# A 2-D spectral filter beside a token MLP: the second transform's radix steps rearranged

## The chip, the cores and the metric

The kernel runs on one core of one Trainium2 chip, as one launch. The metric is the device time in microseconds (us) of a whole execution; the median of three runs is given. The profile is of one execution, and its clock starts at the first recorded instruction.

## The reference, cut to what matters

The input `x` has S = 2048 rows (tokens) and D = 512 columns, in bfloat16.

```python
g = sigmoid((x * gate_w).sum(-1, keepdims=True))
X = rfft2(x.astype(float32)) * (w_r + 1j * w_i)      # 2048 x 257 complex
a = irfft2(X, s=(2048, 512)).astype(bfloat16)
h = layernorm(x)
u = gelu(einsum("bsd,sf->bdf", h, w1) + b1)          # F = 1792
b = (einsum("bdf,fs->bds", u, w2) + b2).transpose(0, 2, 1)
return g * a + (1 - g) * b
```

So there are two branches over the same `x`: a spectral filter (two forward transforms, a product with a complex filter, two inverse transforms) and an MLP over the tokens (two matrix products of 2048 x 1792 x 512 each). A gate per row mixes them.

## The kernel before, in words

**Planner.** Every piece of work is a task with an engine, an estimated duration, what it reads and writes, a priority and the PSUM banks it takes (`Plan`, `add`). A list scheduler (`Plan.order`) runs through time with these estimates and writes out one fixed order for each engine's queue. The chip follows this order; an engine waits at the next instruction until what it reads is there. SP's queue issues nearly all loads and stores.

**MLP.** The first product (`m1`, line 684) accumulates 16 row tiles for each of 14 tiles of F, 512 columns each; ScalarE applies the GELU (line 700). The second (`m2`, line 983) accumulates 14 tiles of F for each of 16 output row tiles; ScalarE or VectorE scale and add them into the output (lines 989, 995, 1001). Weights of the first product stand in a tile `wa` and two tiles `wb`; the second product's weights (14 transfers of 512 KB) are loaded into the same space as it comes free. TensorE is given matmuls of the two products wherever a step of the spectral branch is not ready.

**Spectral branch, forward.** Rows are handled in four residues r of s modulo 4. For each, VectorE does a radix-4 step over row blocks (lines 519 to 526), TensorE multiplies with a cosine and sine table (`fa`, lines 538 to 541; the column d becomes the output's partition, in four blocks `dq`), and ScalarE evicts to the tile `X` (line 544). Then comes the second transform, over the 512 columns. Before the change column d is split as 128 k + p: VectorE does the first radix-4 step over the four blocks k (`d4a`, `d4b`, lines 551 to 558), four instructions for each residue. After that VectorE combines the four residues with a radix-4 step (`radix4`, lines 577 to 590), for each of two halves `lt` of the row frequencies. Half 0 is the special half: one of its columns mixes frequencies and is computed apart with small instructions (`sp0`, `sp1`, lines 602 to 620) and put back into `X` (line 628). Half 1 is combined first.

**Products of the second transform.** For each half, each of four slots `e` and each of two parts c (real and imaginary), a block of four matmuls (`fb`, lines 646 to 649) contracts the partition p: two of 128 columns for the column frequencies 0 and 2 modulo 4, and two of 256 columns that accumulate into one another for the odd ones. That makes 16 blocks. ScalarE evicts each (`fbev`, line 653) into the tile `B` in the order of frequencies. Banks for this come from the two pools `fa` and `fb`, two banks each.

**Filter and inverse.** VectorE prepares small pieces (lines 756 to 793: `wprep`, `c0a`, `c0b`, `nyq`), forms sums and differences (799, 800), multiplies with the filter `W` (807), combines (812 to 821) and does the inverse radix-4 steps (577 to 593). One line goes out by DMA, through a small matmul, and back by DMA. Then the inverse matmuls (`i1`, lines 868 to 875), evictions (881, 883), VectorE sums (891 to 904), the last inverse matmuls (`i3`, lines 942 to 946), evictions with the gate as scale (955) and VectorE's final sums (`es`, lines 964 to 970).

**Gate.** VectorE multiplies `x` with `gate_w` (line 709), ScalarE sums (line 714).

Of the kernel before, what the change touches and what calls it, by code (L numbers as in the profile page):

```python
# [16 lines left out]
P = 128  # L17
S = 2048
D = 512
# [15 lines left out]
def make_tables():  # L35
# [5 lines left out]
    def ang(rows, k, n):  # L41
        return 2 * np.pi * ((rows[..., None] * k) % n) / n
# [42 lines left out]
                    u[:, P] = c[:, P] if lt == 0 else -n[:, P]  # L85
    ti[0, 2816:2945] = np.append(alt, 1.0)

    tb = np.zeros((P, 3, 4, 64))
    i = np.arange(64)
    for b in (0, 2):  # L90
        th = ang(p, b + 4 * i, D)
        tb[:, 0, b // 2] = np.cos(th)
        tb[:, 1, b // 2] = -np.sin(th)
    tb[:, 1, 0, 0] = alt
    tb[:, 2, 0:2] = tb[:, 0, 0:2]
    tc = np.zeros((P, 2, 3, 2, 64))
    for n, b in enumerate((1, 3)):
        th = ang(p, b + 4 * i, D)
        sg = 1.0 if b == 1 else -1.0
        tc[:, 0, 0, n] = np.cos(th)  # L100
        tc[:, 0, 1, n] = -np.sin(th)
        tc[:, 1, 0, n] = -sg * np.sin(th)
        tc[:, 1, 1, n] = -sg * np.cos(th)
    tc[:, :, 2] = tc[:, :, 0]
    cf = np.zeros((P, 4, 2))
    m = np.arange(8).reshape(4, 2)
    for r in range(4):
# [4 lines left out]
            cf[m[2, 0], r, 1], cf[m[3, 0], r, 1] = 1.0, (1.0, -1.0)[r % 2]  # L112
        if r != 0:
            cf[m[2, 1], r, 1], cf[m[3, 1], r, 1] = (0.0, -1.0, 1.0, 1.0)[r], (0.0, -1.0, -1.0, 1.0)[r]
    tb = np.concatenate([tb[:, :, 0:2].reshape(P, 384), tc.reshape(P, 768), cf.reshape(P, 8)], 1)

    tg = np.zeros((P, 642))
    sc = 2.0 / (D * S)
# [21 lines left out]
class Plan:  # L140
# [11 lines left out]
    def add(self, eng, dur, emit, reads=(), writes=(), prio=0.0, alloc=(), free=(), nbytes=0, after=()):  # L152
        t = Task()
        t.eng, t.dur, t.emit, t.prio = eng, dur, emit, prio
        t.alloc, t.free, t.nbytes = tuple(alloc), tuple(free), nbytes
        t.users, t.end, t.ready = [], None, 0.0
        deps = set(after)
        for k in reads:
            if k in self.last_w:
                deps.add(self.last_w[k])  # L160
            self.readers.setdefault(k, []).append(t)
        for k in writes:
            if k in self.last_w:
                deps.add(self.last_w[k])
            deps.update(self.readers.get(k, ()))
            self.last_w[k] = t
            self.readers[k] = []
        deps.discard(t)
        t.deps = deps
        self.tasks.append(t)  # L170
        return t
# [70 lines left out]
def tt(n):  # L242
    return 0.07 + n / 1920.0
# [6 lines left out]
def d1(n):  # L250
    return 0.07 + n / 960.0


def act(n, ptr=0):
    return 0.065 + 0.09 * ptr + n / 1200.0
# [12 lines left out]
def kernel(  # L268
# [77 lines left out]
    def load(key, shape, dt, src, nbytes, prio=0.0):  # L346
        def emit():
            t[key] = sb(shape, dt, key)
            dma(t[key][:], src)
        return add("SP", 0.5, emit, writes=[key], prio=prio, nbytes=nbytes)  # L350
# [52 lines left out]
        dma(t["b1b"][0:NFT], B_b1.rearrange("(t f) -> t f", f=P))  # L403
        dma(t["b2b"][0:4], B_b2.rearrange("(q n) -> q n", q=4))
    add("SP", 1.0, ld_bias, writes=["bias"], prio=7.1, nbytes=16384, after=[a0])
    load("tb", [P, 1160], BF16, tabs["tb"], 296960, prio=9)

    def ld_wb(k, q):
        def emit():
# [46 lines left out]
        dma(t["ti"][:], tabs["ti"])  # L456
    load("tg", [P, 642], BF16, tabs["tg"], 164352, prio=29)


    HACT = set(range(NJ)) - {0, 8, 4}  # L460
    PQ0 = -0.5
    ASTAT = {12, 8}
    for r in range(4):
# [69 lines left out]
        for dq in range(4):  # L533
            def fa(r=r, dq=dq):
                pa = t["pa", r, dq] = ps([P, 2, 2, P], F32, "fa", 2)
                ta = t["ta"][:, r, :]
                w = lambda k: t["xf", r][:, k, dq * P:(dq + 1) * P]
                T.matmul(pa[:, 1], lhsT=w(2), rhs=ta[:, 256:512], start=True, stop=False)  # L538
                T.matmul(pa[:, 1], lhsT=w(3), rhs=ta[:, 384:640], start=False, stop=True)
                T.matmul(pa[:, 0, :, 0:64], lhsT=w(0), rhs=ta[:, 0:128], start=True, stop=True)  # L540
                T.matmul(pa[:, 0, :, 64:128], lhsT=w(1), rhs=ta[:, 128:256], start=True, stop=True)  # L541
            add("PE", mm(128, 128, 256, 256), fa, reads=[("xf", r % 2), ("ta", r)], writes=[("pa", r, dq)], prio=0, alloc=["fa"],
                free=["xf"] if dq == 3 else ())
            add("ACT", act(512), lambda r=r, dq=dq: A.copy(t["X"][:, :, r, :, dq, :], t["pa", r, dq][:]),  # L544
                reads=[("pa", r, dq)], writes=[("X", r, dq)], prio=0, free=["fa"])

        def d4a(r=r):
            xv = t["X"][:, :, r]
            s = t["st"][:, 1024:2048].rearrange("p (a c n) -> p a c n", a=2, c=2)
            two = lambda lo: xv[:, :, :, lo:lo + 2, :].rearrange("p a c j l -> p a c (j l)")  # L550
            V.tensor_add(s, two(0), two(2))
            V.tensor_sub(two(2), two(0), two(2))

        def d4b(r=r):
            xv = t["X"][:, :, r]
            s = t["st"][:, 1024:2048].rearrange("p (a c n) -> p a c n", a=2, c=2)
            V.tensor_add(xv[:, :, :, 0, :], s[:, :, :, 0:P], s[:, :, :, P:2 * P])
            V.tensor_sub(xv[:, :, :, 1, :], s[:, :, :, 0:P], s[:, :, :, P:2 * P])
        add("DVE", 2 * tt(1024), d4a, reads=[], writes=[("X", r, dq) for dq in range(4)] + ["sx"], prio=3.9)
        add("DVE", 2 * tt(512), d4b, reads=["sx"], writes=[("D", r)], prio=3.9)  # L560


    def radix4(view, pq, st, pqk, stk, reads, writes, prio, inverse):
# [56 lines left out]
        V.tensor_add(fx[:, 3, 1], sd[:, 1, 0, 1], sp[:, 2, 1])  # L620
    add("DVE", tiny(12), sp1, reads=["sp"], writes=["fx"], prio=0)

    for lt in (1, 0):
        pr = 3.0 if lt else 3.1
        radix4(lambda lt=lt: t["X"][:, lt].rearrange("p r c j l -> p r c (j l)"),
               lambda: t["xp"][:, 0:2048], lambda: t["st"][:, 0:2048], "xs", "st",
               dk + ([] if lt else ["sp"]), [("Z", lt, 0), ("Z", lt, 1)], pr, False)
    add("DVE", 0.15, lambda: V.tensor_copy(t["X"][:, 0, :, :, :, 0], t["fx"][:]), reads=["fx"],
        writes=[("Z", 0, 0), ("Z", 0, 1)], prio=3.1)

    def tbl(kind, c):
        tb = t["tb"]
        if kind < 2:
            return tb[:, 0:384].rearrange("p (c k i) -> p c k i", c=3, k=2)[:, c:c + 2, kind, :]
        v = tb[:, 384:1152].rearrange("p (g n) -> p g n", g=2)[:, kind - 2]
        return v[:, 128 * c:128 * c + 256]

    for lt in (0, 1):
        for e in (0, 2, 1, 3):
            for c in range(2):  # L640
                tag = ("fa", "fb")[c]

                def fb(lt=lt, e=e, c=c, tag=tag):
                    pb = t["pb", lt, e, c] = ps([P, 2, 4, 64], F32, tag, 2)
                    w = lambda k: t["X"][:, lt, e, c, k, :]
                    T.matmul(pb[:, :, 0, :], lhsT=w(0), rhs=tbl(0, c), start=True, stop=True)
                    T.matmul(pb[:, :, 2, :], lhsT=w(1), rhs=tbl(1, c), start=True, stop=True)
                    for k in (2, 3):
                        T.matmul(pb[:, :, 1::2, :], lhsT=w(k), rhs=tbl(k, c), start=(k == 2), stop=(k == 3))
                add("PE", mm(128, 128, 256, 256), fb, reads=[("Z", lt, e % 2), "tb"], writes=[("pb", lt, e, c)], prio=2, alloc=[tag])  # L650

                def fbev(lt=lt, e=e, c=c):
                    A.copy(t["B"][:, lt, e, 2 * c:2 * c + 2, :].rearrange("p s (i b) -> p s i b", b=4),  # L653
                           t["pb", lt, e, c][:].rearrange("p s b i -> p s i b"))
                add("ACT", act(512), fbev, reads=[("pb", lt, e, c)], writes=[("B", lt, e)], prio=1.8, free=[tag])


    def biasT():
# [105 lines left out]
    for lt in range(2):  # L764
# [8 lines left out]
        if lt == 0:  # L773
            def nyq():
                pz = sb([1, 1280], F32, "X")
                na = pz[:, 0:1024].rearrange("p (i v l) -> p i v l", i=2, v=2)
                nn = t["nn"] = pz[:, 1024:1280].bitcast(BF16).rearrange("p (v l) -> p v l", v=2)
                wn, v = t["wn"], t["B"][0:1, 0, 0, 2:4, :]
                for i in range(2):
                    V.tensor_mul(na[:, i], v, wn[:, i, None, 0:L].to_broadcast([1, 2, L]))  # L780
                V.tensor_sub(nn[:, 0], na[:, 0, 1], na[:, 1, 0])
                V.tensor_add(nn[:, 1], na[:, 1, 1], na[:, 0, 0])
                V.tensor_mul(nn[:, :, 0], t["c0"][0:1, 0, 0, 1, :], wn[:, 0, 0:257:256])
            add("DVE", 3 * d1(512) + 0.1, nyq, reads=bk + [("W", 0), ("W", 1), ("c0", 0)] + pbk, writes=["nn"], prio=0.5)

        def c0b(lt=lt):
            c0, cm, ce, pm = t["c0"][:, lt], t["cm"], t["ce"][:, lt], t["wpm"]
# [46 lines left out]

    def linem():
        pl8 = t["pl8"] = ps([8, D], F32, "fa", 2)
        T.matmul(pl8[:], lhsT=t["tb"][:, 1152:1160], rhs=t["s9"][:], start=True, stop=True)
    add("PE", mm(512), linem, reads=["s9", "tb"], writes=["pl8"], prio=3, alloc=["fa"], after=[combt])
    add("ACT", act(512), lambda: A.copy(t["s8"][:], t["pl8"][:]), reads=["pl8"], writes=["s8"], prio=1.7, free=["fa"])

# [205 lines left out]
```

## Time and profile before

| what | value |
|---|---|
| time, three runs | 132.38, 132.47, 134.06 us, median 132.47 |
| profiled execution | 132.39 us, of which span 130.5 us |
| granted TensorE clock | 0.997 |
| TensorE busy | 125.4 us, 96% |
| VectorE busy | 110.6 us, 85% |
| ScalarE busy | 83.1 us, 64% |
| moved by DMA | 23.18 MB |

The span runs from the first to the last recorded instruction; the execution's time has 1.9 us more around it. A timeline line has start, time, engine, line, operation, output and inputs with their shapes, and in square brackets the idle time of the engine just before and what ended it. Matmuls are pipelined: a recorded matmul of 512 columns lasts 379 ns while the next one starts about 216 ns after it, so distances between starts are what a matmul costs in a stream. The same holds for short VectorE and ScalarE instructions: their starts are closer than their durations.

### The profile page before, as it was taken

How to read it: one execution, taken by the hardware profiler on the slowest of the kernel's cores; microseconds unless marked ns; L12 is line 12 of the kernel's file. 1: busy time of each engine (PE TensorE's matmuls, PEld its weight loads, DVE VectorE, ACT ScalarE, POOL GpSimd, SP SyncE). 2: the span in 40 equal slices, each digit the busy share in tenths (PEclk: the TensorE clock that was granted, in tenths of full speed). 3: DMA queues.
4: the chain of work that ended last, by engine and by line, in shares of the span. 5: the costliest groups of instructions: out<-in, count | busy, mean ns of one | idle time of the engine just before them, and what ended most of it. 6: DMA issues, size and time to landing. Idle time of an engine off the chain costs nothing.

```text
span 130.5 us, 2166 instructions
## 1 busy us (share of the span) xinstructions
PE 125.4 (96%) x780; PEld 70.7 (54%) x780; DVE 110.6 (85%) x248; ACT 83.1 (64%) x166; POOL 0.2 (0%) x4
## 2 busy tenths in 40 slices
PE   6998999999999999999999999999999999999991
PEld 2344565545544484854444555455687577655590
DVE  2689999999999997059999999999959929999961
ACT  4468989599999999996111044322499489962200
POOL 0000000000000000000000000000000000000000
PEclk9999999999999999999999999999999999999998
DMA  4999999943669536799999800000000000312331
GB/s 83 389 372 386 398 394 379 374 91 89 135 184 298 107 85 131 259 288 406 414 421 421 334 6 0 3 5 3 0 0 0 0 5 0 161 69 97 161 121 40
DMA packets 17478, 23.18 MB, mean 178 GB/s; under 512 B 1574, under 2 KB 14908, under 8 KB 17468
## 3 DMA queue, kind: packets, MB, share of 16 engines
q1 hardware_dynamic: 17180, 22.59, 50.6%
q10 hardware_dynamic: 288, 0.46, 1.3%
q8 instruction: 6, 0.10, 0.3%
q14 instruction: 4, 0.03, 0.1%
HBM read 20.93 MB, written 2.10 MB: 176 GB/s over the span
## 4 chain that ended last, share of the span: by engine, by line
PE 58%; DVE 28%; DMA 8%; issue 2%; ACT 2%; SPq 0%; DVEq 0%
PE acc L684 18%; PE acc L983 17%; DMA wa<-in_B_w_dram 5%; PE fb L684 5%; DVE xp L807 3%; DVE st L807 3%; DMA x<-in_A_x_dram 2%; PE fa L684 2%; PE fa L538 2%; DVE xp L812 2%; DVE st L578 2%; DVE B L819 2%; DVE xp L813 2%; PE fb L868 1%; PE fa L868 1%
## 5 line engine op out<-in xcount | busy, mean ns | idle before, releaser
L983 PE MATMUL acc<-gl,wb 128*128 128x512 bf16 (+1 forms) x112 | 27.4, 373 | 0.0
L983 PE MATMUL acc<-gl,wa 128*128 128x512 bf16 (+1 forms) x112 | 27.2, 372 | 0.0
L684 PE MATMUL acc<-h,wb 128*128 128x512 bf16 x112 | 25.9, 379 | 0.0
L989 ACT ACTIVATE x<-acc,ombb,omg 128x512 bf16<-128x512 f32 x14 | 10.8, 785 | 22.7 <-PE acc L983 22.7
L983 PEld LDWEIGHTS <-wb 128*128 128x128 bf16 x126 | 13.4, 114 | 10.3 <-DMA wb<-in_B_w_dram 1.2
L983 PEld LDWEIGHTS <-wa 128*128 128x128 bf16 x126 | 13.5, 114 | 9.4
L684 PE MATMUL acc<-h,wa 128*128 128x512 bf16 x64 | 17.8, 387 | 0.6 <-DVE h L505 0.6
L684 PEld LDWEIGHTS <-wb 128*128 128x128 bf16 x112 | 10.9, 98 | 11.7
L684 PEld LDWEIGHTS <-wa 128*128 128x128 bf16 x112 | 10.4, 99 | 10.8 <-issue 2.1
L700 ACT ACTIVATE gl<-acc,b1f 128x512 bf16<-128x512 f32 x11 | 7.6, 693 | 6.8 <-PE acc L684 6.8
L478 DVE BATCH_NORM_STATS2 stats<-x 128x6 f32<-128x512 bf16 x14 | 9.4, 674 | 2.2 <-DMA x<-in_A_x_dram 2.2
L544 ACT CAST X<-fa 128x512 bf16<-128x512 f32 x16 | 9.3, 582 | 2.7 <-PE fa L541 2.5
L511 ACT ACTIVATE h<-x,nmr,rstd 128x512 bf16<-128x512 bf16 x13 | 9.8, 806 | 0.4 <-DVE nmr L502 0.2
L714 ACT ACTIVATE x<-x 128x512 bf16<-128x512 bf16 x16 | 10.1, 655 | 0.0
L684 PE MATMUL fb<-h,wa 128*128 128x512 bf16 x32 | 9.4, 379 | 0.0
L955 ACT ACTIVATE B<-fb,g 128x512 bf16<-128x512 f32 x8 | 5.9, 735 | 0.0
L955 ACT ACTIVATE B<-fa,g 128x512 bf16<-128x512 f32 x8 | 5.8, 727 | 0.0
L359 PE MATMUL fa<-xp 128*128 128x512 bf16 x10 | 4.4, 632 | 1.2 <-DVE xp L320 1.2
L684 PE MATMUL fa<-h,wa 128*128 128x512 bf16 x16 | 5.6, 379 | 0.0
L653 ACT CAST B<-fb 128x512 bf16<-128x512 f32 x8 | 5.0, 628 | 0.0
L653 ACT CAST B<-fa 128x512 bf16<-128x512 f32 x8 | 4.9, 616 | 0.0
L709 DVE TENSOR_TENSOR x<-x,gw 128x2048 bf16<-128x2048 bf16 x4 | 4.8, 1216 | 0.0
(177 smaller groups left out, 230.0 us busy)
## 6 DMA issues: line engine op xcount, KB each, us to landing
wb<-in_B_w_dram SPq DMA_DIRECT2D x11, 512.0 KB
wa<-in_B_w_dram SPq DMA_DIRECT2D x7, 512.0 KB
wa<-in_B_w_dram SPq DMA_DIRECT2D x3, 896.0 KB
x<-in_A_x_dram SPq DMA_DIRECT2D x3, 512.0 KB
wb<-in_B_w_dram SPq DMA_DIRECT2D x4, 384.0 KB
out_dram<-x SPq DMA_DIRECT2D x3, 512.0 KB
rot<-dft_ti SPq DMA_DIRECT2D x1, 736.5 KB
rot<-dft_ta SPq DMA_DIRECT2D x4, 160.0 KB
```

Source lines behind the costliest of these rows:

```text
L478: V.bn_stats(out=t["stats"][:, j, :], in_=t["x"][:, j // 4, j % 4, :])
L511: add("ACT", 0.71, lambda j=j: A.activation(t["h"][:, j // 4, j % 4, :], t["x"][:, j // 4, j % 4, :], ActF.Identity, bias=t["nmr"][:, j:j ...
L544: add("ACT", act(512), lambda r=r, dq=dq: A.copy(t["X"][:, :, r, :, dq, :], t["pa", r, dq][:]), reads=[("pa", r, dq)], writes=[("X", r, dq ...
L653: A.copy(t["B"][:, lt, e, 2 * c:2 * c + 2, :].rearrange("p s (i b) -> p s i b", b=4), t["pb", lt, e, c][:].rearrange("p s b i -> p s i b"))
L684: T.matmul(t["u", ft][:], lhsT=w[:, j // 4, j % 4, c * P:(c + 1) * P], rhs=t["h"][:, j // 4, j % 4, :], start=(j == jorder[0]), stop=(j == ...
L700: gelus.append(add("ACT", act(512, 1) , lambda ft=ft: A.activation(t["gl"][:, ft, :], t["u", ft][:], ActF.Gelu_apprx_tanh, bias=t["b1f"][: ...
L709: add("DVE", tt(2048), lambda r=r: V.tensor_mul(t["x"][:, :, r, :], t["x"][:, :, r, :], t["gw"][:, None, :].to_broadcast([P, 4, D])), read ...
L714: A.activation(t["x"][:, q, r, :], t["x"][:, q, r, :], ActF.Copy, accum_out=t["glog"][:, 4 * q + r:4 * q + r + 1])
L807: V.tensor_mul(o, xs, w)
L955: A.activation(t["eo", j // 2][:, j % 2], t["i3", j][:], ActF.Copy, scale=t["g"][:, j:j + 1])
L983: T.matmul(t["y", j, n][:, cs], lhsT=w[:, o, 512 * q + r:512 * q + 512:4], rhs=t["gl"][:, ft, cs], start=(ft == 0), stop=(ft == NFT - 1))
L989: A.activation(tbuf(j).rearrange("p h d -> p (h d)"), t["y", j, 0][:], ActF.Identity, bias=t["ombb2"][:, j:j + 1], scale=t["omg"][:, j:j + 1])
```

## The change

Column d is split as 256 h + 2 p + t, with h and t 0 or 1. The first transform takes its stationary operand at every second column, so that its blocks are (h, t). Its evictions go to the scratch tile `xp`, and VectorE does a radix-2 step over h from `xp` to `X` (`d2`), in place of the radix-4 step over k. The products have four matmuls of 128 columns per block, one for each t and each parity of the frequency; each gives cosine and sine parts of 64 frequencies, with which the mirrored frequencies are built as well. The evictions write them interleaved over the products' own operands in `X`, and wait for both blocks of a pair. VectorE then does a radix-2 step over t, from `X` to `B` (`tb2`: three instructions for the even slots of a half, six for the odd ones). The special half is combined first and put first. The table `tb` shrinks from 1160 to 776 columns.

```diff
     load("tb", ...)
-    [P, 1160], 296960 bytes
+    [P, 776], 198656 bytes
...
+    def xe(r):
+        return t["xp"][:, 2048 * r:2048 * r + 2048].rearrange("p (a c j l) -> p a c j l", a=2, c=2, j=4)
...
-                w = lambda k: t["xf", r][:, k, dq * P:(dq + 1) * P]
+                w = lambda k: t["xf", r][:, k, L * (dq // 2) + dq % 2:L * (dq // 2 + 1):2]
...
-            add("ACT", act(512), lambda r=r, dq=dq: A.copy(t["X"][:, :, r, :, dq, :], t["pa", r, dq][:]),
+            add("ACT", act(512), lambda r=r, dq=dq: A.copy(xe(r)[:, :, :, dq, :], t["pa", r, dq][:]),
...
-            V.tensor_add(s, two(0), two(2))
-            V.tensor_sub(two(2), two(0), two(2))
...
-            V.tensor_add(xv[:, :, :, 0, :], s[:, :, :, 0:P], s[:, :, :, P:2 * P])
-            V.tensor_sub(xv[:, :, :, 1, :], s[:, :, :, 0:P], s[:, :, :, P:2 * P])
...
+        def d2(r=r):
+            e, xv = xe(r), t["X"][:, :, r]
+            for i in range(2):
+                V.tensor_add(xv[:, i, :, 0:2], e[:, i, :, 0:2], e[:, i, :, 2:4])
+                V.tensor_sub(xv[:, i, :, 2:4], e[:, i, :, 0:2], e[:, i, :, 2:4])
...
-    for lt in (1, 0):
-        pr = 3.0 if lt else 3.1
+    for lt in (0, 1):
+        pr = 3.0 + 0.1 * lt
...
-                    T.matmul(pb[:, :, 0, :], lhsT=w(0), rhs=tbl(0, c), start=True, stop=True)
-                    T.matmul(pb[:, :, 2, :], lhsT=w(1), rhs=tbl(1, c), start=True, stop=True)
-                    for k in (2, 3):
-                        T.matmul(pb[:, :, 1::2, :], lhsT=w(k), rhs=tbl(k, c), start=(k == 2), stop=(k == 3))
+                    for k in range(4):
+                        T.matmul(pb[:, k % 2, :, k // 2, :], lhsT=t["X"][:, lt, e, c, k, :], rhs=tbl(k, c), start=True, stop=True)
...
-                    A.copy(t["B"][:, lt, e, 2 * c:2 * c + 2, :].rearrange("p s (i b) -> p s i b", b=4),
-                           t["pb", lt, e, c][:].rearrange("p s b i -> p s i b"))
+                    A.copy(t["X"][:, lt, e].rearrange("p c j l -> p (c j l)").rearrange("p (h c g) -> p h c g", h=2, c=2)[:, :, c]
+                           .rearrange("p h (s i b) -> p h s b i", s=2, b=2), t["pb", lt, e, c][:])
...
+            if e >= 2:
+                def tb2(lt=lt, e0=e - 2):
+                    b = t["B"][:, lt]
+                    v = t["X"][:, lt].rearrange("p e c j l -> p e (c j l)").rearrange("p e (h w l) -> p e h w l", h=2, w=4)
+                    bh, vh = b[:, e0::2], v[:, e0::2]
+                    V.tensor_add(bh[:, :, :, 0:P], vh[:, :, 0], vh[:, :, 1])
+                    V.tensor_sub(bh[:, :, 0:4:3, L - 1:P:-1], vh[:, :, 0, 0:4:3, 1:P], vh[:, :, 1, 0:4:3, 1:P])
+                    V.tensor_sub(bh[:, :, 1:3, L - 1:P:-1], vh[:, :, 1, 1:3, 1:P], vh[:, :, 0, 1:3, 1:P])
+                    if e0:
+                        V.tensor_sub(b[:, :, 1:3, 0], v[:, :, 0, 0:4:3, 0], v[:, :, 1, 0:4:3, 0])
+                        V.tensor_copy(b[:, :, 0:4:3, P], v[:, :, 0, 1:3, 0])
+                        V.tensor_copy(b[:, :, 1:3, P], v[:, :, 1, 1:3, 0])
```

In the changed kernel the radix 2 over h stands at lines 545 and 546, the products at line 630, their evictions at line 637 and the radix 2 over t at lines 646 to 652.

More of the change, by code (lines that the diff above doesn't have):

```diff
@@ L86, in make_tables @@
     ti[0, 2816:2945] = np.append(alt, 1.0)
[L88 to L104, printed above, removed]
+    tb = np.zeros((P, 2, 2, 3, 64))
+    for par in range(2):
+        for h in range(2):
+            th = ang(2 * p + h, par + 2 * np.arange(64), D)
+            tb[:, par, h, 0] = np.cos(th)
+            tb[:, par, h, 1] = -np.sin(th)
+            if par == 0:
+                tb[:, 0, h, 1, 0] = (alt, -alt)[h]
+            tb[:, par, h, 2] = tb[:, par, h, 0]
     cf = np.zeros((P, 4, 2))
@@ L114, in make_tables @@
             cf[m[2, 1], r, 1], cf[m[3, 1], r, 1] = (0.0, -1.0, 1.0, 1.0)[r], (0.0, -1.0, -1.0, 1.0)[r]
-    tb = np.concatenate([tb[:, :, 0:2].reshape(P, 384), tc.reshape(P, 768), cf.reshape(P, 8)], 1)
+    tb = np.concatenate([tb.reshape(P, 768), cf.reshape(P, 8)], 1)
     tg = np.zeros((P, 642))
@@ L405 @@
     add("SP", 1.0, ld_bias, writes=["bias"], prio=7.1, nbytes=16384, after=[a0])
-    load("tb", [P, 1160], BF16, tabs["tb"], 296960, prio=9)
+    load("tb", [P, 776], BF16, tabs["tb"], 198656, prio=9)
     def ld_wb(k, q):
@@ L543 @@
                 free=["xf"] if dq == 3 else ())
-            add("ACT", act(512), lambda r=r, dq=dq: A.copy(t["X"][:, :, r, :, dq, :], t["pa", r, dq][:]),
+            add("ACT", act(512), lambda r=r, dq=dq: A.copy(xe(r)[:, :, :, dq, :], t["pa", r, dq][:]),
                 reads=[("pa", r, dq)], writes=[("X", r, dq)], prio=0, free=["fa"])
[L547 to L550, printed above, removed]
-            V.tensor_add(s, two(0), two(2))
-            V.tensor_sub(two(2), two(0), two(2))
-        def d4b(r=r):
-            xv = t["X"][:, :, r]
-            s = t["st"][:, 1024:2048].rearrange("p (a c n) -> p a c n", a=2, c=2)
-            V.tensor_add(xv[:, :, :, 0, :], s[:, :, :, 0:P], s[:, :, :, P:2 * P])
-            V.tensor_sub(xv[:, :, :, 1, :], s[:, :, :, 0:P], s[:, :, :, P:2 * P])
-        add("DVE", 2 * tt(1024), d4a, reads=[], writes=[("X", r, dq) for dq in range(4)] + ["sx"], prio=3.9)
-        add("DVE", 2 * tt(512), d4b, reads=["sx"], writes=[("D", r)], prio=3.9)
+        def d2(r=r):
[3 more added lines that the diff above has]
+                V.tensor_sub(xv[:, i, :, 2:4], e[:, i, :, 0:2], e[:, i, :, 2:4])
+        add("DVE", 4 * tt(512), d2, reads=[("X", r, dq) for dq in range(4)], writes=[("D", r)], prio=3.9)
     def radix4(view, pq, st, pqk, stk, reads, writes, prio, inverse):
@@ L627 @@
                dk + ([] if lt else ["sp"]), [("Z", lt, 0), ("Z", lt, 1)], pr, False)
-    add("DVE", 0.15, lambda: V.tensor_copy(t["X"][:, 0, :, :, :, 0], t["fx"][:]), reads=["fx"],
-        writes=[("Z", 0, 0), ("Z", 0, 1)], prio=3.1)
+        if lt == 0:
+            add("DVE", 0.15, lambda: V.tensor_copy(t["X"][:, 0, :, :, :, 0], t["fx"][:]), reads=["fx"],
+                writes=[("Z", 0, 0), ("Z", 0, 1)], prio=3.0)
     def tbl(kind, c):
[L632 to L636, printed above, removed]
+        return t["tb"][:, 192 * kind + 64 * c:192 * kind + 64 * c + P].rearrange("p (s i) -> p s i", s=2)
     for lt in (0, 1):
@@ L643, in fb @@
                 def fb(lt=lt, e=e, c=c, tag=tag):
[L644 to L647, printed above, removed]
-                    for k in (2, 3):
-                        T.matmul(pb[:, :, 1::2, :], lhsT=w(k), rhs=tbl(k, c), start=(k == 2), stop=(k == 3))
@@ L650 @@
-                add("PE", mm(128, 128, 256, 256), fb, reads=[("Z", lt, e % 2), "tb"], writes=[("pb", lt, e, c)], prio=2, alloc=[tag])
-                def fbev(lt=lt, e=e, c=c):
-                    A.copy(t["B"][:, lt, e, 2 * c:2 * c + 2, :].rearrange("p s (i b) -> p s i b", b=4),
-                           t["pb", lt, e, c][:].rearrange("p s b i -> p s i b"))
-                add("ACT", act(512), fbev, reads=[("pb", lt, e, c)], writes=[("B", lt, e)], prio=1.8, free=[tag])
+                    pb = t["pb", lt, e, c] = ps([P, 2, 2, 2, 64], F32, tag, 2)
@@ new lines, in fb @@
+                    for k in range(4):
+                        T.matmul(pb[:, k % 2, :, k // 2, :], lhsT=t["X"][:, lt, e, c, k, :], rhs=tbl(k, c), start=True, stop=True)
+                add("PE", mm(128, 128, 128, 128), fb, reads=[("Z", lt, e % 2), "tb"], writes=[("pb", lt, e, c)], prio=2, alloc=[tag])
+            for c in range(2):
+                tag = ("fa", "fb")[c]
+                def fbev(lt=lt, e=e, c=c):
+                    A.copy(t["X"][:, lt, e].rearrange("p c j l -> p (c j l)").rearrange("p (h c g) -> p h c g", h=2, c=2)[:, :, c]
+                           .rearrange("p h (s i b) -> p h s b i", s=2, b=2), t["pb", lt, e, c][:])
+                add("ACT", act(512), fbev, reads=[("pb", lt, e, i) for i in range(2)], writes=[("R", lt, e, c)], prio=1.8, free=[tag])
@@ new lines @@
+            if e >= 2:
[10 more added lines that the diff above has]
+                        V.tensor_copy(b[:, :, 1:3, P], v[:, :, 1, 1:3, 0])
+                es_ = (e - 2, e) if e == 2 else (0, 1, 2, 3)
+                add("DVE", tt(1024) + 2 * tt(508) + tiny(3) * (e > 2), tb2, reads=[("R", lt, i, c) for i in (e - 2, e) for c in range(2)],
+                    writes=[("B", lt, i) for i in es_], prio=2.5)
@@ L783, in nyq @@
                 V.tensor_mul(nn[:, :, 0], t["c0"][0:1, 0, 0, 1, :], wn[:, 0, 0:257:256])
-            add("DVE", 3 * d1(512) + 0.1, nyq, reads=bk + [("W", 0), ("W", 1), ("c0", 0)] + pbk, writes=["nn"], prio=0.5)
+            add("DVE", 3 * d1(512) + 0.1, nyq, reads=[("B", i, e) for i in range(2) for e in range(4)] + [("W", 0), ("W", 1), ("c0", 0)] + pbk, writes=["nn"], prio=0.5)
         def c0b(lt=lt):
@@ L836, in linem @@
         pl8 = t["pl8"] = ps([8, D], F32, "fa", 2)
-        T.matmul(pl8[:], lhsT=t["tb"][:, 1152:1160], rhs=t["s9"][:], start=True, stop=True)
+        T.matmul(pl8[:], lhsT=t["tb"][:, 768:776], rhs=t["s9"][:], start=True, stop=True)
     add("PE", mm(512), linem, reads=["s9", "tb"], writes=["pl8"], prio=3, alloc=["fa"], after=[combt])
```

## The prediction

> **What bounds the kernel now.** First the busy times and slices of the page, to see which engine has no idle time.
>
> ```profile
> span 130.5 us, 2166 instructions
> ...
> PE 125.4 (96%) x780; PEld 70.7 (54%) x780; DVE 110.6 (85%) x248; ACT 83.1 (64%) x166; POOL 0.2 (0%) x4
> ...
> PE   6998999999999999999999999999999999999991
> ...
> DVE  2689999999999997059999999999959929999961
> ```
>
> TensorE is busy in every slice, and a busy figure can hide a slow stream, so the PE timeline is read next: how far apart do the matmuls start?
>
> ```profile
> 45.42 0.22 PE L646 MATMUL fa<-tb,X 128*128 128x128 bf16 x1
> 45.48 0.22 PE L647 MATMUL fa<-tb,X 128*128 128x128 bf16 x1
> 45.53 0.38 PE L649 MATMUL fa<-tb,X 128*128 128x256 bf16 x2
> 45.75 0.22 PE L646 MATMUL fb<-tb,X 128*128 128x128 bf16 x1
> ...
> 104.70 0.22 PE L942 MATMUL fa<-tg,xp 128*128 128x129 bf16 x1
> ...
> 105.82 0.38 PE L983 MATMUL acc<-gl,wa 128*128 128x512 bf16 x1
> ...
> 116.75 1.67 PE L983 MATMUL acc<-gl,wb 128*128 128x512 bf16 x7
> 118.26 1.67 PE L983 MATMUL acc<-gl,wa 128*128 128x512 bf16 x7
> ```
>
> One block of the second transform takes 0.33 us (45.42 to 45.75). Between 104.70 and 105.82 stand twenty matmuls of 127 to 129 columns: 0.056 us each. Seven matmuls of 512 columns take 1.51 us, 0.2155 each. Starts lie as close as columns allow, almost everywhere, so the end is set by the number of columns that TensorE streams. Work taken from it shortens the span, if its fixed order never waits. Two other views show who could make it wait, the DVE timeline and that of the weight loads.
>
> ```profile
> 51.40 0.25 DVE L628 CAST X<-fx 128x32 bf16<-128x32 f32 x1
> 56.51 0.17 DVE L770 CAST c<-B 128x8 f32<-128x8 bf16 x1 [4.86 <-ACT B L653]
> ...
> 126.03 0.48 DVE L1001 SCALAR_TENSOR_TENSOR x<-acc,omg,x 128x256 bf16<-128x256 f32 x1 [0.75 <-PE acc L983]
> ```
>
> ```profile
> 69.74 0.11 PEld L983 LDWEIGHTS <-wb 128*128 128x128 bf16 x1 [0.30 <-DMA wb<-in_B_w_dram]
> ...
> 70.97 0.11 PEld L983 LDWEIGHTS <-wb 128*128 128x128 bf16 x1 [0.43 <-DMA wb<-in_B_w_dram]
> ```
>
> VectorE is nearly full, but stands idle 4.86 us while ScalarE evicts the special half, and at the end it has 0.75 us to spare before TensorE's last outputs. At 69 to 71 us the second MLP product uses weight tiles the moment they land.
>
> **The products, TensorE.** Each of 16 blocks loses its two 256-column matmuls for two of 128. Four of 128 at 0.056 make 0.224 for 0.33: 0.106 x 16 = 1.70 us off the path. The operands of the first transform are now read at stride 2 as weights; the inverse transform's weights (L868) are read at stride 2 already and load in 98 ns, as do contiguous ones (98 ns at L538): nothing. The nearest bound from the other side is that one 98 ns load per matmul could not be hidden: 4 x 0.098 = 0.39 per block, +1.0 us. I take 0.056, since all twenty matmuls above have such a load each.
>
> The Trainium skill speaks against this edit: TensorE: Matmul & The Clock Gate, section Back-to-back issue gap, gives about 81 ns for each of a sustained stream of weight load and 128-column matmul. By it a block would keep 0.324 us, and TensorE would gain an estimated 0.1 us. The trace has 56 ns in such a stream and does not agree.
>
> **VectorE.** The old radix 4 over column blocks takes two instructions of 1024 and two of 512 elements per row residue: 2.00 us from start to start (25.19 to 27.46, less 0.27 of other work). The new radix 2 takes four of 512, at 0.335 (L557, L558): 1.34. Four residues: -2.6 us. Added is the radix 2 over t behind the products, four times: one of 1024 (0.60, as L583) and two of 508 (0.335 start to start, as L967 and L968, which also read from an odd element and one of which writes backwards), and twice three tiny ones of 0.075: 4 x 1.27 + 0.45 = 5.5 us. Net +2.9 us on an engine with 19.9 us idle.
>
> Where does it fall? The built order puts all four L709 multiplies ahead of the last residue's radix 2, and three 512-column matmuls more ahead of that residue's last block (35.59 + 0.65 = 36.24), so its eviction ends near 37.4 and the radix 2 near 38.85, where the old one ended at 40.00. From 40.00 to the first product with the filter (63.81) VectorE is busy 18.3 us and idle 5.5, all waits for evictions. With the special half first, the evictions run from 46 to 54 while VectorE still has the other half's radix 4, so the idle time fills: 38.85 + 18.3 + 5.5 = 62.65, 1.15 us earlier than before. From there the chain is unchanged, so its end comes 1.15 earlier, with 0.75 to spare before: it stays behind TensorE for a gain up to 1.9.
>
> **The special half first.** TensorE reaches the first block after the same 77 matmuls of the first MLP product, at 45.42. It now needs the special column as well: 38.85 + 0.2 copy + 1.0 (twelve tiny ones) + 2.27 + 1.2 + 1.2 (radix 4) + 0.35 (column put back) = 45.07. Cover 0.35 us; without it TensorE and all MLP matmuls queued behind stand still, one for one.
>
> **Evictions.** Still 16 of 512, now waiting for both blocks of a pair (0.22 us, once), as they overwrite the products' operands. They start 0.477 apart (L653, 45.95 to 49.29). The 5th to 8th block need banks at 46.75, 47.19, 47.63 and 48.07, freed at 46.6, 47.1, 47.55 and 48.03: 0 to 0.2 us of waits. New is that each writes every second element. No row has such a write. Bounds: 0.477 from L653, which reads as scattered, and 0.71 from L989, the dearest of that size (three in 2.12). I take L653, the same engine, size and source.
>
> The Trainium skill has a price for the stride: SBUF — State Buffer, section Door 1: The DMA port swizzle, has 16-byte lines and full speed from two hits a line on; two-byte values at stride 2 hit four times, so by it the eviction costs nothing more. No run here shows it yet.
>
> **Transfers.** SP issues the same list in the same order; the table is 98 KB smaller, at 390 GB/s (the page's early slices) 0.25 us. But the tiles of the second weight matrix come at the pace of the DMA engines (busy share 0.94 to 1.0 from 53 to 74 us), whatever TensorE does. It would start that product at 68.02 - 1.70 = 66.32. The built order uses the second wb tile as its 14th matmul, at 69.12; that tile let go at 69.74 before. Waits of 0.4 to 0.7 us against 0.2 before (31 matmuls took 6.87, not 6.68): -0.2 to -0.5 of the gain, 0.35 taken. Behind that tile everything on TensorE queues, so it is not made up. The inverse transform needs VectorE and the line sent back by DMA (90.8 at the latest by the shift of 1.15, TensorE there at about 92): covered.
>
> **Sum.** 1.70 - 0.35 = 1.35 us. The profiled execution took 132.39 (span 130.5 and 1.9 around it): 131.04. The median is 0.08 above the profiled one: 131.1.
>
> **Rivals.** First, *waits eat the gain*: TensorE's fixed order waits for the radix 4 at 45.4 and 51.6 (cover 0.35 and 0.2), for banks, and for tiles. For it: all covers are below 0.4. Against: the order was moved along with the work. With 0.5 at each of two places, 132.1.
>
> Second, the other side, *slow interleaved evictions make VectorE the bound*. The third of the added radix-2 steps needs twelve evictions and one activation, done at 52.3, where VectorE can take it at 52.65. If a write at stride 2 takes twice the time (0.95), they are done at 58.0, VectorE's chain comes 5.35 later less 1.15, and past its 0.75 to spare the end goes to 132.4 + 4.2 - 0.75 = 135.9. VectorE decides from 0.56 us an eviction, and the kernel is slower than before from 0.67. At L989's 0.71 it is 0.5 slower: 132.9. For it: nothing measured writes so. Against: ScalarE's 512-element rows differ only by 0.1 with layout (L544 to L653).
>
> Third, *weight loads pace the products*, so the change does not do what it says: 132.4 + 1.0 = 133.4. Against: the twenty matmuls.
>
> By the 81 ns of the Trainium skill (TensorE: Matmul & The Clock Gate, Back-to-back issue gap) this third way would give an estimated 132.3.
>
> **Chances.** Forecast 0.62 (own range 130.4 to 131.7); waits 0.17; evictions 0.13, of which 0.09 past 2%; weight loads 0.04; a gain beyond 2% 0.04, for waits that the trace hides. Two per cent of the median is 2.65 us, about what a measurement of this kernel can tell from no change. So faster 0.04, slower 0.10 (evictions 0.09 and 0.01 for weight loads with waits on top), within 0.86. The range runs from 130.3 (no wait at all is 130.7, plus the table's 0.25 and a little) to 133.4.
>
> **What would show it.** Right: products 0.056 apart; evictions still 0.477 apart and ending near 54.5; no VectorE idle time of several us between 39 and 63; filter products from about 62.6; first wb tiles waited for about 0.5 us; TensorE ending 1.3 us sooner. Wrong: eviction groups above 700 ns mean, 508-element steps far above 0.42, PE rows with waits for VectorE, or VectorE busy to the last store.

## The result, and the profile after

The changed kernel takes 133.68 us (median of 17 runs, 133.53 to 133.91) against 132.46 before (17 runs): a ratio of 1.0085, 95% interval 1.007 to 1.0101. It is slower by 1.2 us, where 131.1 was forecast and 133.4 was the end of the range. That is within the 2% by which the prediction tells faster and slower apart, and yet clear of noise: the interval is 0.15% (0.2 us) wide on each side. The top of its page:

```profile
span 131.7 us, 2172 instructions
...
PE 124.1 (94%) x766; PEld 69.6 (53%) x780; DVE 113.8 (86%) x266; ACT 84.9 (64%) x166; POOL 0.2 (0%) x4
...
PE   6899999999999999869999999999999999999991
```

TensorE has less to do and the span is longer: the 17th and 18th of the 40 slices (52.7 to 59.3 us) show 8 and 6 tenths where the kernel before had nines. That is the stretch of the products and their evictions. The PE timeline of the changed kernel there (idle time in brackets):

```profile
45.65 0.39 PE L630 MATMUL fa<-tb,X 128*128 128x128 bf16 x4
45.87 0.39 PE L630 MATMUL fb<-tb,X 128*128 128x128 bf16 x4
...
54.58 0.39 PE L630 MATMUL fb<-tb,X 128*128 128x128 bf16 x4 [0.35 <-ACT X L637]
...
57.39 0.38 PE L736 MATMUL fb<-wt,flip 128*128 128x256 bf16 x2 [0.92 <-ACT X L637]
...
69.52 1.68 PE L983 MATMUL acc<-gl,wa 128*128 128x512 bf16 x7
```

A block takes 0.22 us as forecast. But TensorE waits for ScalarE to free banks. From the first product to the second MLP product (45.65 to 69.52) it needs 23.87 us for work of 20.68 (16 blocks of 0.222, 77 matmuls at 0.2155, and an estimated 0.54 for the filter's flips): 3.2 us lost. Before, 45.42 to 68.02 held work of 22.41, and 0.2 was lost. So 1.7 us of work was saved and 3.0 us of waits came. Another 0.2 came ahead of the first product (45.65 for 45.42), so that the second MLP product starts 1.5 us later. Behind that point 0.3 comes back: the last group of matmuls starts at 128.21 for 127.00, 1.2 us later.

The page's groups of evictions (this one and its twin from the pool `fa`, of 778 ns) and the ScalarE timeline of the changed kernel show who is late:

```profile
L637 ACT CAST X<-fb 128x512 bf16<-128x512 f32 x8 | 6.3, 784 | 1.5 <-DVE B L648 1.5
```

```profile
46.23 0.75 ACT L637 CAST X<-fa 128x512 bf16<-128x512 f32 x1
46.81 0.76 ACT L637 CAST X<-fb 128x512 bf16<-128x512 f32 x1
...
49.13 0.81 ACT L637 CAST X<-fb 128x512 bf16<-128x512 f32 x1
...
52.62 0.74 ACT L637 CAST X<-fa 128x512 bf16<-128x512 f32 x1 [0.30 <-DVE X L577]
...
54.36 0.76 ACT L637 CAST X<-fa 128x512 bf16<-128x512 f32 x1
56.61 0.73 ACT L637 CAST X<-fb 128x512 bf16<-128x512 f32 x1 [1.49 <-DVE B L648]
```

Two things are seen. Evictions start 0.58 apart, not 0.477. And ScalarE stands still for VectorE, in the middle of them. The VectorE timeline has the other side:

```profile
49.97 0.69 DVE L646 TENSOR_TENSOR B<-X 128x1024 bf16<-128x1024 bf16 x1 [1.09 <-ACT X L637]
...
55.16 0.69 DVE L646 TENSOR_TENSOR B<-X 128x1024 bf16<-128x1024 bf16 x1 [1.09 <-ACT X L637]
...
56.10 0.42 DVE L648 TENSOR_TENSOR B<-X 128x508 bf16<-128x508 bf16 x1
```

The first radix-2 step over t reads slots 0 and 2, which evictions 1 to 4 write; the fourth ends at 48.76 (47.97 + 0.79). The step starts at 49.97, when the sixth ends (49.13 + 0.81), which writes slot 1. The third step, of the other half, starts at 55.16, when the 13th ends (54.36 + 0.76), again slot 1. In return the 14th, slot 1 too, waits until that step's last instruction ends (56.10 + 0.42). No value passes between them. The reading is that the program's waits take a slice of every second slot as all that lies between its first and its last, so that a step over slots 0 and 2 and an eviction into slot 1 wait for one another; a run below tests it. The 11th eviction (slot 2) waits likewise for the radix 4 that writes slots 1 and 3 (L577, done at 51.85 + 0.69).

### The profile page after: what moved, and what is told of

Its sections match the earlier page's. It is cut to its first block, busy times and chain, and to the rows that moved or that the text cites. A ratio compares the mean times of both kernels' runs of the same rounds, so it can differ in the third digit from the quotient of the medians.

```text
span 131.7 us, 2172 instructions
## 1 busy us (share of the span) xinstructions
PE 124.1 (94%) x766; PEld 69.6 (53%) x780; DVE 113.8 (86%) x266; ACT 84.9 (64%) x166; POOL 0.2 (0%) x4
## 4 chain that ended last, share of the span: by engine, by line
PE 70%; ACT 17%; DVE 6%; DMA 2%; issue 1%; ACTq 0%
PE acc L983 35%; PE acc L684 17%; ACT X L637 5%; ACT x L714 4%; ACT gl L700 4%; PE fb L684 3%; DMA x<-in_A_x_dram 2%; PE fa L684 2%; PE fa L533 2%; ACT xp L539 2%; PE fb L868 1%; PE fa L868 1%; DVE B L646 1%; PE fa L534 1%; ACT W L740 1%
## 5 line engine op out<-in xcount | busy, mean ns | idle before, releaser
L684 PE MATMUL acc<-h,wb 128*128 128x512 bf16 x108 | 25.3, 379 | 0.2
L684 PE MATMUL acc<-h,wa 128*128 128x512 bf16 x61 | 17.2, 389 | 0.8 <-DVE h L500 0.6
L539 ACT CAST xp<-fa 128x512 bf16<-128x512 f32 x16 | 9.3, 580 | 3.0 <-PE fa L536 2.8
L637 ACT CAST X<-fb 128x512 bf16<-128x512 f32 x8 | 6.3, 784 | 1.5 <-DVE B L648 1.5
L637 ACT CAST X<-fa 128x512 bf16<-128x512 f32 x8 | 6.2, 778 | 0.3 <-DVE X L577 0.3
L630 PEld LDWEIGHTS <-X 128*128 128x128 bf16 x64 | 4.4, 97 | 3.3 <-issue 2.3
```

Source lines behind the costliest of these rows:

```text
L539: add("ACT", act(512), lambda r=r, dq=dq: A.copy(xe(r)[:, :, :, dq, :], t["pa", r, dq][:]), reads=[("pa", r, dq)], writes=[("X", r, dq)], ...
L630: T.matmul(pb[:, k % 2, :, k // 2, :], lhsT=t["X"][:, lt, e, c, k, :], rhs=tbl(k, c), start=True, stop=True)
L637: A.copy(t["X"][:, lt, e].rearrange("p c j l -> p (c j l)").rearrange("p (h c g) -> p h c g", h=2, c=2)[:, :, c] .rearrange("p h (s i b) - ...
L684: T.matmul(t["u", ft][:], lhsT=w[:, j // 4, j % 4, c * P:(c + 1) * P], rhs=t["h"][:, j // 4, j % 4, :], start=(j == jorder[0]), stop=(j == ...
```

## The experiments

Theory A: TensorE's fixed order waits for banks, for two separate reasons, the slower eviction and these waits between neighbours. Theory B, the rival: VectorE's longer chain costs the time. That TensorE's waits are for banks is read from what ended them, ScalarE's evictions; no run gave the products more banks. All runs of one group shared the runs of the kernel before (medians 132.45 and 132.47).

**Evictions that write in one piece.** Only the eviction's order of elements is changed: PSUM is now read scattered.

```diff
-    .rearrange("p h (s i b) -> p h s b i", s=2, b=2), t["pb", lt, e, c][:])
+    .rearrange("p h (s i b) -> p h s i b", s=2, b=2), t["pb", lt, e, c][:].rearrange("p h s b i -> p h s i b"))
```

> The changed kernel, but its 16 evictions of the products read PSUM scattered and write SBUF in one piece, instead of reading in one piece and writing every second element; the values and the orders of all queues stay the same. Theory A (the lost time is TensorE waiting for banks in its fixed order, for two reasons: each eviction costs 0.58 instead of 0.477 us, and the radix 2 over t and the evictions wait for one another where they touch different slots): starts of evictions 0.477 apart again, TensorE's loss between the first product and the first matmul of the second MLP product falls from 3.2 to about 1.5 us, time 131.8 to 132.4. Theory B (the longer VectorE chain is what costs): evictions may be faster, but the time stays at 133.3 or above.

Measured: 132.44 us, ratio 0.9999 (0.9989 to 1.001), 1.24 us less than the changed kernel and just above the 131.8 to 132.4 that was expected. Evictions start 0.477 apart. TensorE's loss is 1.9 us, more than the 1.5 expected; the waits between neighbours stay. ScalarE's timeline of this run:

```profile
46.85 0.63 ACT L637 CAST X<-fb 128x512 bf16<-128x512 f32 x1
47.33 0.64 ACT L637 CAST X<-fa 128x512 bf16<-128x512 f32 x1
...
52.11 0.59 ACT L637 CAST X<-fa 128x512 bf16<-128x512 f32 x1 [0.74 <-DVE X L577]
...
55.74 0.59 ACT L637 CAST X<-fb 128x512 bf16<-128x512 f32 x1 [1.49 <-PE fa L736]
```

The second wait is put down to TensorE's L736 here. That matmul, started at 55.33, writes other banks than this eviction reads; the eviction's own block was started at 52.21. VectorE's last instruction of the step over slots 0 and 2 ends at 55.65, just ahead of 55.74:

```profile
55.23 0.42 DVE L648 TENSOR_TENSOR B<-X 128x508 bf16<-128x508 bf16 x1
```

**Neighbouring slots.** The forward radix 4 writes its results in the order 0, 2, 1, 3, so that a step over t reads two slots that lie side by side.

```diff
-            V.tensor_sub(dst(4, 1), p, q)
+            V.tensor_sub(dst(4 if inverse else 2, 1), p, q)
...
-                V.tensor_add(dst(2, 5), s, ur)
-                V.tensor_sub(dst(3, 3), sr, u)
+                V.tensor_add(dst(4, 3), s, ur)
+                V.tensor_sub(dst(5, 1), sr, u)
...
-                    bh, vh = b[:, e0::2], v[:, e0::2]
+                    bh, vh = b[:, e0::2], v[:, 2 * e0:2 * e0 + 2]
```

The products and the evictions use slot 2 (e % 2) + e // 2 as well, and the special column is put back accordingly.

> The changed kernel, but the forward radix 4 puts slot 2 next to slot 0 and slot 3 next to slot 1, so that the radix 2 over t reads two neighbouring slots and no longer spans the slot between them; evictions still write every second element. Theory A: the waits of ScalarE for VectorE (1.49 and 0.30 us) and of VectorE for the fifth, sixth and thirteenth eviction go, evictions stay 0.58 apart, time 132.2 to 133.0. Theory B: 133.3 or above.

Measured: 131.86 us, ratio 0.9949 (0.9935 to 0.9964), 1.82 less than the changed kernel and a little better than expected. The evictions that waited run through, still 0.58 apart; these two in the ScalarE timeline are the 13th and the 14th:

```profile
53.79 0.88 ACT L641 CAST X<-fa 128x512 bf16<-128x512 f32 x1
54.36 0.90 ACT L641 CAST X<-fb 128x512 bf16<-128x512 f32 x1
```

**Both edits.**

> The changed kernel with both of these edits. Theory A: what was forecast for the change comes out, 130.8 to 131.5, with TensorE's loss between the first product and the second MLP product below 0.6 us and waits for the second weight matrix of about 0.4 us in their place. Theory B: the time stays above 132.9, since VectorE has the same work.

Measured: 130.63 us (130.38 to 130.79), ratio 0.9854 (0.9835 to 0.9873). This is 1.8 us (1.5%) faster than the kernel before, within the 2% but clear of noise, a little better than expected, and 3.05 faster than the changed one; the two edits alone gave 1.24 and 1.82, which add up to 3.06. Theory A holds and B falls: VectorE has the same work as in the changed kernel. The waits of 0.4 us for the second weight matrix that were expected did not come. Lines of this run's PE and weight-load timelines, one fence each:

```profile
45.90 0.39 PE L634 MATMUL fa<-tb,X 128*128 128x128 bf16 x4
...
66.68 1.67 PE L989 MATMUL acc<-gl,wa 128*128 128x512 bf16 x7
```

```profile
68.09 0.11 PEld L989 LDWEIGHTS <-wb 128*128 128x128 bf16 x1 [0.22 <-DMA wb<-in_B_w_dram]
```

| kernel | evictions apart | TensorE lost, 1st product to 2nd MLP product | filter products from | time |
|---|---|---|---|---|
| before | 0.477 | 0.2 | 63.81 | 132.46 |
| changed | 0.58 | 3.2 | 65.33 | 133.68 |
| in one piece | 0.477 | 1.9 | 64.16 | 132.44 |
| neighbouring slots | 0.58 | 1.3 | 63.87 | 131.86 |
| both | 0.477 | 0.1 | 62.82 | 130.63 |

**The eviction's write in the kernel before.** There the frequencies are interleaved by four.

```diff
-    A.copy(t["B"][:, lt, e, 2 * c:2 * c + 2, :].rearrange("p s (i b) -> p s i b", b=4),
-           t["pb", lt, e, c][:].rearrange("p s b i -> p s i b"))
+    A.copy(t["B"][:, lt, e, 2 * c:2 * c + 2, :].rearrange("p s (i b) -> p s b i", b=4), t["pb", lt, e, c][:])
```

> The kernel before, but its 16 evictions of the products read PSUM in one piece and write every fourth element of SBUF, instead of the other way round. Theory A: the cost of an eviction follows the write, so starts are 0.58 apart or more instead of 0.477, and the kernel loses some of the 1.7 us that ScalarE needs more: 132.8 to 133.8. If the cost belongs to something else in the changed kernel (an access in more dimensions, or writing over the products' operands), evictions stay at 0.477 and the time at 132.4.

Measured: 142.7 us, ratio 1.077 (1.075 to 1.079), far beyond what theory A expected: the direction is the expected one, the size is not. The ScalarE timeline:

```profile
46.93 1.40 ACT L653 CAST B<-fb 128x512 bf16<-128x512 f32 x1
48.06 1.41 ACT L653 CAST B<-fa 128x512 bf16<-128x512 f32 x1
49.21 1.40 ACT L653 CAST B<-fb 128x512 bf16<-128x512 f32 x1
```

At every fourth element an eviction takes 1.14 us from start to start, 2.4 times the one in one piece. Sixteen of them cost ScalarE 10.6 us more, and the kernel pays 10.2. The cost belongs to the write, not to the changed kernel's place or dimensions: the edit in the changed kernel kept both and came back to 0.477.

**The special half last again,** with both edits.

```diff
-    for lt in (0, 1):
-        pr = 3.0 + 0.1 * lt
+    for lt in (1, 0):
+        pr = 3.1 - 0.1 * lt
```

> The kernel with both edits, but with the special half combined last again, as before the change. Theory A: this step is worth something only as cover: VectorE again waits some microseconds for the last evictions, and since its chain has no spare time left at the end, the kernel is 0.5 to 2 us slower than with both edits, 131.1 to 132.6. If the order of the halves does not matter, 130.5 to 130.8.

Measured: 134.88 us, ratio 1.0197 (1.0173 to 1.0221): 4.25 us slower than both edits with the special half first, twice what was expected at most. The planner makes new orders here, so the step is measured together with what else moves by it. VectorE's timeline:

```profile
56.54 0.69 DVE L650 TENSOR_TENSOR B<-X 128x1024 bf16<-128x1024 bf16 x1 [3.87 <-ACT X L641]
58.50 0.69 DVE L650 TENSOR_TENSOR B<-X 128x1024 bf16<-128x1024 bf16 x1 [0.59 <-ACT X L641]
...
129.42 0.34 DVE L1007 SCALAR_TENSOR_TENSOR x<-fb,omg,x 128x128 bf16<-128x128 f32 x1
```

VectorE waits 4.5 us for evictions, its filter products start at 66.96 instead of 62.82, and at the end it works without a pause to 129.8, while TensorE's last group starts at 125.45, as in the run with both edits (125.37). Here VectorE sets the end.

**The special half first, alone,** in the kernel before.

```diff
-    for lt in (1, 0):
-        pr = 3.0 if lt else 3.1
+    for lt in (0, 1):
+        pr = 3.0 + 0.1 * lt
```

The special column is put back right after its own half, as in the change.

> The kernel before with this one step of the change: the special half combined first and put first. Theory A: VectorE's wait of 4.86 us for evictions shrinks and its filter products start earlier than 63.81, but TensorE's columns set the end, so the time stays within 0.4 of 132.45. If VectorE's chain were what sets the end, it would fall by a microsecond or more.

Measured: 132.22 us, ratio 0.9996 (0.997 to 1.0022): no difference. VectorE's longest wait there shrinks from 4.86 to 1.56 us and its filter products start at 61.84, but the time stays, as it should where TensorE sets the end. The step is worth nothing where VectorE has time to spare, and about 4 us where it has none.

**One addition of VectorE twice,** with both edits.

```diff
-                    V.tensor_add(bh[:, :, :, 0:P], vh[:, :, 0], vh[:, :, 1])
+                    for _ in range(2):
+                        V.tensor_add(bh[:, :, :, 0:P], vh[:, :, 0], vh[:, :, 1])
```

> The kernel with both edits, with the 1024-element addition of each of the four radix-2 steps over t done twice (the second time over the same values): 2.4 us more for VectorE, nothing else. It measures what VectorE has to spare. If VectorE's work is hidden as the forecast had it (spare up to about 0.5 us at the end), the time rises by 1.5 to 2.4, to 132.1 to 133.0; if VectorE still has several microseconds to spare, it stays at 130.6 to 131.0.

Measured: 133.52 us, ratio 1.0082 (1.0068 to 1.0096), 2.9 more than without for 2.4 us of work, somewhat above what was expected. The PE timeline shows where it surfaces, at the inverse transform:

```profile
93.40 0.22 PE L879 MATMUL fa<-rot,B 128*128 128x129 bf16 x1 [1.53 <-DMA B<-s]
...
96.36 0.23 PE L879 MATMUL fb<-rot,B 128*128 128x128 bf16 x1 [0.97 <-DVE B L580]
```

TensorE waits 2.5 us, for the line sent back by DMA (itself behind VectorE) and for the inverse radix 4. With both edits alone, the DVE and PE timelines show the same radix 4 and the matmul behind it:

```profile
93.07 0.68 DVE L580 TENSOR_TENSOR B<-st 128x1024 bf16<-128x1024 bf16 x1
```

```profile
93.81 0.23 PE L878 MATMUL fb<-rot,B 128*128 128x128 bf16 x1
```

The radix 4 ends at 93.75 and the matmul starts at 93.81: TensorE and VectorE are due together there, and VectorE has nothing to spare. The matmul is 2.55 us later with the doubled addition (96.36 for 93.81), and the two profiled executions are 2.6 apart (133.40 and 130.79). The 2.9 of the medians has 0.3 more only because these two executions lie at the near ends of their runs.

## Why the prediction was wrong, by its steps

**The products (1.70 us): right.** Blocks of 0.22 us. The first sixteen of the 64 matmuls, in one stream with a weight load each, take 0.89 us (45.65 to 46.54), 0.0555 us each; the 81 ns of the Trainium skill (TensorE: Matmul & The Clock Gate, Back-to-back issue gap) is not what this kernel shows.

**VectorE's work: right.** The radix 2 over h took 1.34 us (25.24 to 26.58), the steps over t 0.60 and twice 0.335, the special column was put back at 45.1 to 45.35 where 45.07 was worked out, ahead of the first product at 45.65. (The prediction's 77 matmuls of the first MLP product are those behind the first product; 147 stand ahead of it, in both kernels.) With both edits the filter products start at 62.82; 62.65 was forecast.

**The evictions: this step failed, twice.** First the price: 0.477 was taken from L653 since it was nearest, and it is 0.58 when every second element is written. The bounds of 0.477 and 0.71 held it, and the prediction's own sign of being wrong, eviction groups above 700 ns mean, came true at 778 and 784. The rival on the other side named the slow write. But it gave 0.67 us as the point from which the kernel is slower, through VectorE's end, while at 0.58 the loss already came, through banks. For those the prediction had 0 to 0.2 us of waits and counted the 5th to 8th block alone. By its own figures TensorE's fixed order had 0.04 to 0.15 us to spare at each of these, and 0.1 us more for each eviction runs through this in the first two. The edit that takes this reason away gains 1.24 us. The Trainium skill's rule (SBUF — State Buffer, Door 1: The DMA port swizzle), by which two hits in a 16-byte line already give full speed, let the stride look free. The runs do not agree: 0.1 us more with four hits in a line, 0.66 more with two.

Second, what waits for what: the prediction counted that an eviction now waits for both blocks of a pair, but not that the new VectorE steps and the evictions share the tile `X`, with slots 0 and 2 on one side and slot 1 between them on the other. The edit that takes it away gains 1.82 us, the larger part, and no rival had it. "Waits eat the gain" named banks and the radix 4 and had 0.5 us at each of two places; TensorE's waits were 3 us more than before.

**The tiles of the second weight matrix (0.35): wrong, but not what decided.** In the changed kernel TensorE came too late to wait for them. With both edits it came at 66.68, where 66.32 was forecast. One weight load stood 0.22 us there, but the matmuls did not: the first seven end their stream at 68.19 (66.68 + 7 x 0.2155), where the next starts. So the term is nothing, and the 0.2 us that the kernel before loses there is gone too. Without this term the forecast's sum is 130.7; the kernel with both edits has 130.63. That these agree so closely is partly luck. In the profiled execution TensorE reached the first product 0.48 us later than before (45.90), of which 0.25 came in a wait for a bias transfer (L666, at 21.51). It made most of this up, 0.1 between that product and the second MLP product and 0.3 behind it, of which 0.2 at the tiles.

**VectorE's spare time: right in size, not in place.** The prediction had it behind TensorE for a gain up to 1.9 us, by the 0.75 us at the end, and called the inverse transform covered. At a gain of 1.8 the doubled addition shows none left, but at the inverse transform. The kernel before had no cover there either; its PE timeline:

```profile
94.78 0.23 PE L872 MATMUL fb<-rot,B 128*128 128x128 bf16 x1 [0.17 <-DVE B L593]
```

So the 1.9 came out close by luck.

**The special half first: right that it fills VectorE's idle time.** Its worth once the waits are gone, some 4 us, was not given by the prediction.

## What to carry to other kernels

When an engine's work moves from one place to another, price what the moved data do to the write side of the engine between, not only the engines at both ends: here the saving on TensorE was real and was lost at ScalarE's evictions. Where two engines work on one tile in turns, lay out the parts so that each access covers one run of neighbouring parts; here a strided slice waited for, and held up, what lay in between, at 1.82 us. A fixed order with covers of a tenth of a microsecond has no room for a surprise of that size: 0.1 us on each of 16 evictions cost this kernel 1.24.

## What the runs showed of the hardware

The cost of a ScalarE eviction of 512 values from PSUM depends on how it writes bfloat16 to SBUF: 0.477 us from start to start in one piece, 0.58 at every second element, 1.14 at every fourth. Reading PSUM scattered costs nothing measurable: such an eviction takes 0.477 when its write is in one piece, and L740 of the changed kernel, which reads in one piece and writes in runs of 256, takes 0.46 (39.85 to 40.31). For these evictions a scattered access belongs on the reading side.

TensorE's matmuls of 128 columns, each with its own weight load, start 0.0555 to 0.056 us apart whether their output lies in one piece (104.70 to 105.82 before) or in runs of 64 columns (45.65 to 46.54 after).
